# Attention and a two-layer network on one core: a new order of all engines, drawn with at most eight loads open, and one V load moved ahead of a K and a Q

## The chip, the cores and the metric

The kernel runs on one core of a Trainium2 chip. The metric is the device time of one execution in microseconds. Engines are called TensorE (PE, matmuls; PEld are its weight loads), VectorE (DVE), ScalarE (ACT), GpSimd (POOL) and SyncE (SP). All loads are issued by GpSimd, which converts float32 to float16 on the way; all stores are issued by SyncE, and some of the last by ScalarE too.

## The reference

Eight batches of attention with 12 heads, 448 tokens and 64 columns a head, then a network of two layers over the 3584 tokens:

```
scores = q @ k.T / sqrt(64);  attn = softmax(scores);  x = attn @ v     # 8 x 12 x (448, 64)
x = x laid out as (3584, 768)
h = x @ w_in            # w_in (768, 2048)
g = h * sigmoid(h)
out = g @ w_out         # w_out (2048, 768), out (3584, 768) float32
```

## The kernel before

**Work.** The 12 heads of a batch form three groups of four. A unit is a group of a batch; batch 0's groups are cut into two pieces of query tokens (7 times 32 each), so there are 6 + 21 = 27 units, numbered in that order (units 0 to 2 are the first pieces of batch 0, 3 to 5 the second ones, 6 to 8 the groups of batch 1). For each unit:

- K and Q are loaded (L322, L332) and transposed in 32 x 32 blocks on VectorE (L387, L398).
- Scores (L406): four heads side by side in four row tiles of 32 of the array, one chunk of keys at a time, into PSUM.
- Exponentials on ScalarE (L442), into tiles E.
- Sums over keys: VectorE adds tiles of E (L453), TensorE multiplies with ones (L483, or L497 in batch 0), VectorE transposes, inverts and spreads the sums (L542, L559, L570).
- E times V (L468) in column tiles of 32, and VectorE's scaling into xT (L607).

The first layer is computed block by block (L620), its gate by a tanh on ScalarE (L641) and a product on VectorE (L666). The last four batches are taken as two pairs with seven products instead of eight (L756), with additions on VectorE (L789) and ScalarE's copies and gates (L783, L802). The second layer is direct for the first four half tiles (L850, here called plain) and by seven products of sums for the rest (L837), with additions on VectorE (L829 for the operands, L890 for the results, L662 for sums of `w_out`).

On TensorE matmuls thus come in several tile shapes: full (128 x 128), column tiles of 32, row tiles of 32, and a few with 64. Until the first block of the first layer, matmuls with zeros (L1773) fill gaps that the plan foresees.

**What sets the order.** All instructions are written out by a planner. `Order` holds a clock, the time at which each engine is free, and lists of waiting operations for ScalarE and VectorE; each operation has a duration, dependencies and a bias. At each step ScalarE and VectorE take the ready operation with the lowest ready time plus bias; TensorE takes scores, attention or network blocks by rules of the main loop. When all is planned, the operations are emitted in order of planned start, and every engine runs its list in that order. The planned times thus decide the order, but the chip waits for semaphores, not for the plan.

**Loads.** `Order.load` estimates how long a load takes by its rows and bytes, with fixed extras for certain loads (`DMA_GAPS`, `more`). GpSimd's list is a queue in the order in which `plan_k`, `plan_q`, `plan_v`, `plan_w_in` and `plan_w_out` are called; its head waits in the plan for a free buffer only:

```
op.done = self.dma_free + DMA_TAIL          # planned landing
...
plan_k(1, 2)
plan_q(NB0 + 2)
for hg in range(NG):
    plan_v(1, hg, hg + 1)
plan_w_out(NFF // 2, 3 * NFF // 4)
```

In the built program of before, loads use eight semaphores in turn: every load from the ninth on waits until the load eight places before it has landed. This is so in both kernels. V of a unit is loaded in four pieces, by rows of 32 partitions (L352).

Of the kernel before, what the change touches and what calls it, by code (L numbers as in the profile page):

```python
# [18 lines left out]
HOP = 0.10  # L19
DMA_ROW = 0.004  # L20
DMA_RATE = 13400.0
DMA_GAPS = {1: 0.3, 3: 1.4}
FETCH = 5.6
DMA_START = 1.2
DMA_TAIL = 1.0


# [4 lines left out]
def act(n):  # L32
    return n * 0.000824 + 0.177


class Ring:


    def __init__(self, n, names=None):
        self.free = [(0.0, x) for x in (range(n) if names is None else names)]  # L40
# [54 lines left out]
class Order:  # L95


    def __init__(self, shy):
        self.now, self.shy = 0.0, shy
        self.free = {"PE": 1.0, "ACT": 2.1, "DVE": 1.2, "POOL": 1.2}  # L100
        self.wait = {"ACT": [], "DVE": []}
        self.pool = []
        self.dma_free, self.loads = 0.0, 0
        self.pe_n, self.fetched = 0, 0.0
        self.out = []
        self.mode, self.moe_mode = None, "full"
        self.steps = []
        self.busy = {e: 0.0 for e in self.free}
# [44 lines left out]
    def next_step(self):  # L153
        self.on_pe(self.steps.pop(0), self.moe_mode)

    def load(self, rows, row_bytes, emit, ring=None, gate=None, more=0.0):
        op = Op("POOL", 0.58, emit)
        self.loads += 1
        took = rows * (DMA_ROW + row_bytes / DMA_RATE) / 16 + DMA_GAPS.get(self.loads, more)
        self.pool.append((op, took, ring, gate))  # L160
        return op

    def step(self):

        soon = []
        for eng in ("ACT", "DVE"):
            if self.free[eng] > self.now:
                soon.append(self.free[eng])
                continue
            best, urgent = None, None  # L170
            for op in self.wait[eng]:
                at = op.ready()
                if at is None:
                    continue
                if at > self.now:
                    soon.append(at)
                    if op.bias <= -10 and (urgent is None or at < urgent):
                        urgent = at
                elif best is None or at + op.bias < best[0]:
                    best = (at + op.bias, op)  # L180
            if best and best[1].bias >= 0 and eng == "DVE" and urgent is not None:
                if urgent < self.now + self.shy * best[1].busy:
                    continue
            if best:
                self.wait[eng].remove(best[1])
                self.start(best[1])
                soon.append(self.free[eng])
        if self.free["POOL"] > self.now:
            soon.append(self.free["POOL"])
        elif self.pool:  # L190
            op, took, ring, gate = self.pool[0]
            at = 0.0
            if ring is not None:
                at = ring.when(1)
            if at is not None and gate is not None:
                g = gate()
                at = None if g is None else max(at, g)
            if at is not None and at <= self.now:
                self.pool.pop(0)
                if ring is not None:  # L200
                    ring.take()
                self.start(op)
                self.dma_free = max(self.dma_free, self.now + DMA_START) + took
                op.done = self.dma_free + DMA_TAIL
                soon.append(self.free["POOL"])
            elif at is not None:
                soon.append(at)
        return soon
# [3 lines left out]
def kernel(  # L212
# [13 lines left out]
    DFF = moe_w_in.shape[1]  # L226
    HG = 4
    NG = NH // HG
# [8 lines left out]
    NFF = DFF // 128  # L237
# [13 lines left out]
    COLD = 8.5  # L251
    FIRST = 47
    WHOLE = 7
    TANH_B = -2
    GATE_B = -6
    ADD_B = 1
    SUM_B = -3
    COPY_B = -2
    READ_B = -6
    PAIR_B = -6  # L260
    SILU_B = -1
    HOLD = 0.2
    TILED = 5
    QUART = 1
    JOIN = 0
    STRIPS = 80.0
    VFIRST = 3
    TURN = 4
    LOOK = 1
    SOON = -5  # L270
    KEEP = 0.3
    NBD = 3
    SHY = 0.5
    TWB = 8
    SXB = 8
    SURE = -1.3
    PIECES = ((0, 7), (7, TPP))
# [42 lines left out]
    def load_k(b, hg):  # L320
        t = sb.tile([128, TPP * D], FP16, name=f"rk_{b}_{hg}", tag="rk", bufs=NRK)
        nc.gpsimd.dma_start(out=t, in_=group_of(k, b, hg))  # L322
        rawk[(b, hg)] = t
# [36 lines left out]
    def load_w_in(c, f0, f1):  # L360
        nc.gpsimd.dma_start(
            out=w_in_t[:, 2 * c : 2 * c + 2, f0:f1],
            in_=moe_w_in[256 * c : 256 * (c + 1), f0:f1].rearrange(
                "(p j) f -> p j f", j=2
            ),
        )
# [552 lines left out]
    units = []  # L919
# [5 lines left out]
    od = Order(SHY)  # L925
# [7 lines left out]
    def plan_k(b, hg):  # L933
        ld_k[(b, hg)] = od.load(128, 2 * D * TPP, lambda: load_k(b, hg), rk_ring)

    def plan_q(n):
        g0, g1 = units[n][2:]
        ring = rq_ring if g0 == 0 else None
        ld_q[n] = od.load(128, 2 * D * (g1 - g0), lambda: load_q(n), ring)

    def plan_v(b, hg0, hg1):
        made = []
        for x in range(4):
            ring = v_ring if (x == 0 and b > 0) else None
            heads, toks = HG * (hg1 - hg0), X_TOK[form(b, hg0)][x][1]
            made.append(
                od.load(32 * heads, 2 * D * toks, lambda x=x: load_v(b, hg0, hg1, x), ring)
            )
        for hg in range(hg0, hg1):
            ld_v[(b, hg)] = made  # L950

    def plan_w_in(f0, f1):
        made = [
            od.load(256, 2 * (f1 - f0), lambda c=c: load_w_in(c, f0, f1), more=0.7 * (f0 + c == 0))
            for c in range(NG)
        ]
        for f in range(f0 // 128, f1 // 128):
            ld_win[f] = made

    def plan_w_out(f0, f1):  # L960
        wout_rows.append(f0)
        ld_wout.append(od.load(128 * (f1 - f0), 2 * DM, lambda: load_w_out(f0, f1)))

    NB0 = NG * len(PIECES)
    for hg in range(NG):
        if hg == VFIRST:
            plan_v(0, 0, 1)
        plan_k(0, hg)
        plan_q(hg)
    plan_v(0, int(VFIRST < NG), NG)  # L970
    plan_q(NG)
    if QUART:
        plan_w_in(0, DFF // 4)
        plan_q(NG + 1)
        plan_q(NG + 2)
        plan_w_in(DFF // 4, DFF // 2)
    else:
        plan_q(NG + 1)
        plan_q(NG + 2)
        plan_w_in(0, DFF // 2)  # L980
    plan_k(1, 0)
    plan_q(NB0)
    if QUART:
        plan_w_in(DFF // 2, 3 * DFF // 4)
        plan_w_in(3 * DFF // 4, DFF)
    else:
        plan_w_in(DFF // 2, DFF)
    plan_k(1, 1)
    plan_q(NB0 + 1)
    plan_w_out(0, NFF // 4)  # L990
    plan_w_out(NFF // 4, NFF // 2)
    plan_k(1, 2)
    plan_q(NB0 + 2)
    for hg in range(NG):
        plan_v(1, hg, hg + 1)
    plan_w_out(NFF // 2, 3 * NFF // 4)
    plan_w_out(3 * NFF // 4, NFF)
    for n in range(NB0 + NG, NU):
        b, hg = units[n][:2]
        plan_k(b, hg)  # L1000
        plan_q(n)
        plan_v(b, hg, hg + 1)

    turned = {"n": 0}

# [36 lines left out]
    def queue_ffn1(b, g0, g1):  # L1042
# [6 lines left out]
        for fs in turns:  # L1049

            def run(fs=fs):
# [4 lines left out]
                for i, f in enumerate(fs):  # L1056
# [15 lines left out]
                        [op],  # L1072
                        -3 if b == 0 else TANH_B,
                        tail=0.2,
# [42 lines left out]
    def plan_pair():  # L1117
        for todo in pair_todo[:8]:
# [9 lines left out]
            if qk_seq or od.pool or not e_ring.can(1, od.now):  # L1128
# [8 lines left out]
                    [pair_w[(k, f0)] for k in {2: (1,), 4: (2,)}.get(m, ())],  # L1137
                    TWB + f0,
                )
# [43 lines left out]
    def queue_pair_f(pb, f, xs):  # L1183
# [10 lines left out]

        def read(name, eng, fn, deps, then=None, bias=PAIR_B):
            busy = act(S) + 0.04 if eng == "ACT" else S / 960.0 + 0.155
# [5 lines left out]
        def gate_of(j, r, x, deps, then):  # L1202
            read((j, r), "ACT", lambda: silu(pb, f + HF * j, r, x), deps + silu_op, then, SILU_B)
            g_op.setdefault((pb + r, f + HF * j), []).append(done[(j, r)])
# [136 lines left out]
    def plan_sums():  # L1341
# [12 lines left out]
        for m in (5, 6, 7, 3):  # L1354
            sg_op[(qd, m)] = []
            n = HF if qd < WHOLE else HF // 2
            for f0 in range(0, HF, n):
                deps = [x for f in range(f0, f0 + n) for x in gates[f] + gates[f + HF]]
                if m != 5:
# [7 lines left out]
                            deps,  # L1367
                            SUM_B,
                        )
# [95 lines left out]
    def moe_ready():  # L1465

        soon, held = None, 0
        if av_data["at"] is not None and av_data["at"] <= od.now + HOLD:
            held = len(av_seq[0][0]) if av_seq[0][1] else 1
        if qk_data["at"] is not None and qk_data["at"] <= od.now + KEEP:  # L1470
            held += 1
# [315 lines left out]
    while True:  # L1787
# [9 lines left out]
        if od.free["PE"] <= od.now:  # L1797
# [8 lines left out]
            if qk is not None and qk <= od.now and (od.now >= pace["next"] or moe_i is None):  # L1806
                u0 = units[qk_seq[0][0][0]]
# [32 lines left out]
        if zb is not None and warm["on"] and od.free["PE"] <= od.now and wait > 0.06 and od.now > 0.9:  # L1840
            rate = 2350.0 if od.now > COLD else 1200.0
            n = int(wait * rate / 64) * 64 if od.now > COLD else int(wait * rate / 64 + 0.9) * 64
            if warm.pop("first", None):
                n = FIRST * 128
            n = max(n, 64)
            op = Op("PE", n / rate, lambda n=n, at=zb: run_zeros(n, at))
# [37 lines left out]
```

## Time and profile before

| what | value |
|---|---|
| median of 3 runs | 388.33 us (387.20 to 390.61) |
| the profiled execution | 386.79 us |
| its span in the trace | 385.0 us |
| TensorE busy | 377.3 us (98% of the span) |
| VectorE busy | 297.2 us (77%) |
| ScalarE busy | 244.1 us (63%) |
| GpSimd busy (issuing loads) | 88.0 us (23%) |
| granted TensorE clock | 0.994 on average |
| loads | 22.8 MB on GpSimd's queue |

The durations used below come from this one profiled execution, so sums are made against its own 386.79 us. Busy shares are averages over stages: start-up (to about 22 us), batch 0 and the loading of both weight matrices (to about 75 us), attention of the other batches between network blocks (to about 245 us), and the paired batches with the last products (to the end). Starts of matmuls are recorded, their ends are modelled. In brackets at the end of a timeline line stand the idle time of the engine ahead of that instruction and what ended it. A line such as L352 is a line of the kernel before; where the change shifts lines, the same operation stands 7 lines further down ahead of the planning part and 12 lines further up behind it.

### The profile page before, as it was taken

The page shows a single profiled execution, that of the slowest core. Times are in us where ns is not written, and L with a number is a line of the kernel's source. Part 1 is how long each engine was busy: PE and PEld are TensorE (multiplying, and loading weights), DVE is VectorE, ACT ScalarE, POOL GpSimd, SP SyncE. Part 2 cuts the span into 40 slices and gives each one's busy share as a digit, 9 for nine tenths or more (in the row PEclk, how much of TensorE's full clock was granted, in tenths as well). Part 3 has the DMA queues.
Part 4 walks back from the last instruction along what each step waited for, and adds up shares of the span by engine and source line. Part 5 has one row for each costly group of instructions (what it writes and reads, how often), then busy time and mean ns, then how long its engine had stood idle before and what let it go on. Part 6 is the DMA issues. An engine that isn't in the chain of part 4 may idle for free.

```text
span 385.0 us, 12240 instructions
## 1 busy us (share of the span) xinstructions
PE 377.3 (98%) x5184; PEld 197.6 (51%) x5184; DVE 297.2 (77%) x549; ACT 244.1 (63%) x381; POOL 88.0 (23%) x159
## 2 busy tenths in 40 slices
PE   7999998999999999999999999999999999999996
PEld 3567763444444444445444445555556655555663
DVE  2558677898889898898978788989788647777662
ACT  3888895798868588886667978136871037872000
POOL 7564364602324426050335000000000000000000
PEclk9899999999999999999999999999999999999999
DMA  7999999951919596447594301120002330001343
GB/s 116 200 206 208 171 157 211 145 100 21 127 33 168 90 173 83 65 62 113 104 179 59 48 3 44 44 66 16 2 0 68 94 84 5 0 2 43 94 105 90
DMA packets 37222, 34.61 MB, mean 90 GB/s; under 512 B 11696, under 2 KB 37168, under 8 KB 37168
## 3 DMA queue, kind: packets, MB, share of 16 engines
q0 software_dynamic: 26416, 22.82, 40.1%
q1 hardware_dynamic: 9984, 10.24, 9.8%
q10 hardware_dynamic: 768, 0.79, 0.8%
q8 instruction: 40, 0.66, 0.7%
q14 instruction: 14, 0.11, 0.1%
HBM read 45.61 MB, written 11.01 MB: 147 GB/s over the span
## 4 chain that ended last, share of the span: by engine, by line
PE 86%; DMA 8%; DVE 2%; POOL 1%; issue 1%; ACT 0%; ACTq 0%; POOLq 0%
PE P L837 31%; PE P L756 16%; PE P L620 15%; PE P L406 10%; PE P L468 9%; DMA rq<-in_q_dram 8%; PE P L850 2%; PE P L1773 2%; PE P L483 1%; POOL V L352 1%; PE P L497 0%; DMA out_dram<-ost 0%; POOL rk L322 0%; DVE G L666 0%; DVE rq L398 0%
## 5 line engine op out<-in xcount | busy, mean ns | idle before, releaser
L442 ACT ACTIVATE E<-P 128x448 f16<-128x448 f32 (+4 forms) x172 | 153.1, 918 | 49.1 <-PE P L406 47.5
L620 PE MATMUL P<-xT,w_in_t 128*32 128x448 f16 (+2 forms) x1236 | 82.1, 339 | 0.0
L352 POOL DMA_DIRECT2D V<-in_v_dram x84 | 46.1, 562 | 90.0 <-PE P L468 65.9
L620 PEld LDWEIGHTS <-w_in_t 128*32 128x32 f16 (+1 forms) x1236 | 45.2, 97 | 34.2 <-issue 14.7
L837 PEld LDWEIGHTS <-G 128*32 128x32 f16 (+1 forms) x928 | 39.7, 97 | 27.9 <-issue 4.8
L406 PE MATMUL P<-rq,KT 32*128 32x448 f16 (+4 forms) x864 | 51.0, 342 | 2.3 <-DVE rq L398 2.0
L666 DVE SCALAR_TENSOR_TENSOR G<-G,P 128x448 f16<-128x448 f16 x64 | 38.4, 607 | 12.0 <-ACT G L641 11.2
L837 PEld LDWEIGHTS <-S 128*32 128x32 f16 (+1 forms) x648 | 30.9, 97 | 21.7 <-issue 2.7
L837 PE MATMUL P<-D,G 128*32 128x384 f16 (+1 forms) x448 | 38.9, 326 | 0.0
L837 PE MATMUL P<-w_out_t,S 128*32 128x384 f16 (+1 forms) x424 | 38.9, 326 | 0.0
L641 ACT ACTIVATE G<-P 128x448 f16<-128x448 f32 x64 | 34.6, 544 | 2.6 <-PE P L620 1.9
L890 DVE TENSOR_TENSOR ost<-P,u 128x384 f32<-128x384 f32 x39 | 21.5, 551 | 18.8 <-PE P L837 15.7
L837 PE MATMUL P<-w_out_t,G 128*32 128x384 f16 (+1 forms) x480 | 35.0, 327 | 0.0
L468 PE MATMUL P<-E,V 128*32 128x448 f16 (+2 forms) x672 | 34.9, 355 | 0.0
L756 PE MATMUL P<-sx,tw 128*128 128x448 f16 x144 | 30.8, 352 | 0.0
L406 PEld LDWEIGHTS <-KT 32*128 32x128 f16 (+2 forms) x864 | 14.6, 99 | 29.1 <-issue 25.8
L756 PEld LDWEIGHTS <-tw 128*128 128x128 f16 x192 | 18.8, 98 | 17.5
L607 DVE SCALAR_TENSOR_TENSOR xT<-P,R 128x448 f16<-128x448 f32 x42 | 24.2, 614 | 4.2 <-PE P L468 4.0
L387 DVE STREAM_TRANSPOSE KT<-rk 128x256 f32<-128x256 f32 (+3 forms) x48 | 16.6, 383 | 10.6 <-DMA rk<-in_k_dram 8.8
L468 PEld LDWEIGHTS <-V 128*32 128x32 f16 (+2 forms) x672 | 14.7, 95 | 18.9 <-issue 10.4
L894 ACT COPY u<-P 128x384 f32<-128x384 f32 x13 | 6.2, 479 | 26.1 <-PE P L837 21.1
L453 DVE TENSOR_TENSOR T<-T,E 128x1792 f16<-128x1792 f16 x20 | 21.7, 1083 | 0.4
(80 smaller groups left out, 450.6 us busy)
## 6 DMA issues: line engine op xcount, KB each, us to landing
out_dram<-ost SPq DMA_DIRECT2D x208, 48.0 KB, 1.7
rk<-in_k_dram POOLq DMA_DIRECT2D x24, 224.0 KB, 5.4
rq<-in_q_dram POOLq DMA_DIRECT2D x21, 224.0 KB, 5.5
w_in_t<-in_moe_w_in_dram POOLq DMA_DIRECT2D x12, 256.0 KB, 8.7
w_out_t<-in_moe_w_out_dram POOLq DMA_DIRECT2D x4, 768.0 KB, 11.4
V<-in_v_dram POOLq DMA_DIRECT2D x43, 64.0 KB, 3.9
V<-in_v_dram POOLq DMA_DIRECT2D x40, 48.0 KB, 4.2
out_dram<-ost ACTq DMA_DIRECT2D x16, 48.0 KB, 1.8
```

Source lines behind the costliest of these rows:

```text
L352: nc.gpsimd.dma_start(out=VT[(b, hg0)][32 * x : 32 * (x + 1), :, 0:count, :], in_=v[b, hs].rearrange("h (i g) d -> i h g d", g=TPP)[:, :, ...
L406: nc.tensor.matmul(out=P[p0 : p0 + 32 * (x1 - x0), pS[h], at : at + nq], lhsT=KT[(b, hg)][32 * h : 32 * (h + 1), c, x0:x1, :, e], rhs=QT[n ...
L442: nc.scalar.activation(out=E[(n, w)][0:kr, h0:h1, 0:nk], in_=P[0:kr, bank : bank + h1 - h0, 0:nk], func=AF.Exp, scale=attn_scale,)
L453: nc.vector.tensor_tensor(out=T[n], in0=T[n] if step else E[(n, 0)], in1=E[(n, step + 1)], op=ALU.add,)
L468: nc.tensor.matmul(out=a[32 * h : 32 * (h + 1), 0:nq], lhsT=w, rhs=e[k0:k1, h, at : at + nq], start=start, stop=stop, skip_group_check=True,)
L607: nc.vector.scalar_tensor_tensor(out=xc(b, cc)[:, 32 * g0 : 32 * g1], in0=acc[(n, part)][:, 0:nq], scalar=0.5, in1=rdn_t[n].rearrange("p g ...
L620: nc.tensor.matmul(out=h_t[(b, f, t0)][m0:m1, 0 : t1 - t0], lhsT=w_in_t[:, cc, 128 * f + m0 : 128 * f + m1], rhs=xc(b, cc)[:, t0:t1], star ...
L641: nc.scalar.activation(out=g, in_=h, func=AF.Tanh)
L666: nc.vector.scalar_tensor_tensor(out=g, in0=g, scalar=1.0, in1=h, op0=ALU.add, op1=ALU.mult)
L756: nc.tensor.matmul(out=pp_t[(*key, PBANK[m])], lhsT=w[:, c, :], rhs=xc(pb + x[0], 3 * x[1] + c) if isinstance(x, tuple) else sx_t[(pb, x)] ...
L837: nc.tensor.matmul(out=pr_t[(qd, BANK[m])][m0:m1, 0:OH], lhsT=w[:, f, m0:m1], rhs=W_[m][:, f, :], start=(f == 0 and BANK[m] == m), stop=(f ...
L890: nc.vector.tensor_tensor(out=out, in0=a, in1=b, op=op)
```

## The change

The planner's picture of the loads is replaced. `Order.load` keeps every load in a list; a load may be issued in the plan only 0.28 us after the load eight places before it has landed (`LANES`, `LANE`). The fixed extras of single loads give way to pauses at six planned times (`DMA_PAUSES`), and a load of more than 128 rows begins later by 0.0044 us for each further row. The order of the loads is written as a list, in which `u` stands for K and Q of a unit (Q alone for units 3 to 5), `v` for V, `i` for a quarter of `w_in` and `o` for a quarter of `w_out`. Read against the order before, one item has moved: `v3`, V of batch 1's first group, stands ahead of `u8`, that batch's last K and Q, not behind it. Some biases change: tanh -2 to -1, sums of the second layer's operands -3 to 1, additions of the pairs -6 to -2, gates of the pairs -1 to -0.3, sums of `w_in` for the pairs 8 to 4, and two margins for holding PSUM banks (`HOLD`, `KEEP`) become 0. Since all of this feeds the planner, the order on every engine is another one from about 47 us on; what is computed is the same.

```diff
-DMA_GAPS = {1: 0.3, 3: 1.4}
+DMA_PAUSES = ((0.0, 0.3), (4.0, 1.35), (15.5, 0.9), (21.0, 0.7), (48.5, 0.8), (65.0, 0.8))
+LANES = 8
+LANE = 0.28
+DMA_START_ROW = 0.0044
...
-    def load(self, rows, row_bytes, emit, ring=None, gate=None, more=0.0):
+    def load(self, rows, row_bytes, emit, ring=None):
         op = Op("POOL", 0.58, emit)
-        self.loads += 1
-        took = rows * (DMA_ROW + row_bytes / DMA_RATE) / 16 + DMA_GAPS.get(self.loads, more)
-        self.pool.append((op, took, ring, gate))
+        n = len(self.loads)
+        self.loads.append(op)
+        took = rows * (DMA_ROW + row_bytes / DMA_RATE) / 16
+        lane = self.loads[n - LANES] if n >= LANES else None
+        begin = DMA_START + DMA_START_ROW * max(0, rows - 128)
+        self.pool.append((op, took, ring, lane, begin))
         return op
...
-            if at is not None and gate is not None:
-                g = gate()
-                at = None if g is None else max(at, g)
+            if at is not None and lane is not None:
+                at = None if lane.done is None else max(at, lane.done + LANE)
             if at is not None and at <= self.now:
...
-                self.dma_free = max(self.dma_free, self.now + DMA_START) + took
+                self.dma_free = max(self.dma_free, self.now + begin)
+                while self.pauses and self.pauses[0][0] <= self.dma_free:
+                    self.dma_free += self.pauses.pop(0)[1]
+                self.dma_free += took
                 op.done = self.dma_free + DMA_TAIL
...
-    TANH_B = -2
+    TANH_B = -1
...
-    SUM_B = -3
+    SUM_B = 1
...
-    PAIR_B = -6
-    SILU_B = -1
-    HOLD = 0.2
+    PAIR_B = -2
+    SILU_B = -0.3
+    HOLD = 0
...
+    LOADS = "u0 u1 u2 v0 u3 i0 u4 u5 i1 u6 i2 i3 u7 o0 o1 v3 u8 v4 v5 o2 o3"
...
-    KEEP = 0.3
+    KEEP = 0
...
-    TWB = 8
+    TWB = 4
...
+    rest = LOADS.split()
     for n in range(NB0 + NG, NU):
-        b, hg = units[n][:2]
-        plan_k(b, hg)
-        plan_q(n)
-        plan_v(b, hg, hg + 1)
+        rest += [f"u{n}", f"v{n - NG}"]
+    for what in rest:
+        plan(what)
```

The calls in the plan of before that this list takes the place of are left out here, as is `plan`, which calls `plan_k`, `plan_q`, `plan_v`, `plan_w_in` or `plan_w_out` by an item's letter.

More of the change, by code (lines that the diff above doesn't have):

```diff
@@ L102, in __init__ @@
         self.pool = []
-        self.dma_free, self.loads = 0.0, 0
+        self.dma_free, self.loads, self.pauses = 0.0, [], list(DMA_PAUSES)
         self.pe_n, self.fetched = 0, 0.0
@@ L190, in step @@
         elif self.pool:
-            op, took, ring, gate = self.pool[0]
+            op, took, ring, lane, begin = self.pool[0]
             at = 0.0
@@ L253 @@
     WHOLE = 7
-    TANH_B = -2
+    TANH_B = -1
     GATE_B = -6
     ADD_B = 1
-    SUM_B = -3
+    SUM_B = 1
     COPY_B = -2
     READ_B = -6
-    PAIR_B = -6
-    SILU_B = -1
-    HOLD = 0.2
+    PAIR_B = -2
+    SILU_B = -0.3
+    HOLD = 0
     TILED = 5
-    QUART = 1
     JOIN = 0
     STRIPS = 80.0
-    VFIRST = 3
+    LOADS = "u0 u1 u2 v0 u3 i0 u4 u5 i1 u6 i2 i3 u7 o0 o1 v3 u8 v4 v5 o2 o3"
     TURN = 4
@@ L953, in plan_w_in @@
         made = [
-            od.load(256, 2 * (f1 - f0), lambda c=c: load_w_in(c, f0, f1), more=0.7 * (f0 + c == 0))
+            od.load(256, 2 * (f1 - f0), lambda c=c: load_w_in(c, f0, f1))
             for c in range(NG)
@@ L964, with plan @@
     NB0 = NG * len(PIECES)
[L965 to L997, printed above, removed]
+    def plan(what):
+        kind, at = what[0], int(what[1:])
+        if kind == "u":
+            b, hg = units[at][:2]
+            if at < NG or b:
+                plan_k(b, hg)
+            plan_q(at)
+        elif kind == "v":
+            plan_v(at // NG, at % NG, NG if at == 0 else at % NG + 1)
+        elif kind == "i":
+            plan_w_in(DFF // 4 * at, DFF // 4 * (at + 1))
+        else:
+            plan_w_out(NFF // 4 * at, NFF // 4 * (at + 1))
+    rest = LOADS.split()
     for n in range(NB0 + NG, NU):
-        b, hg = units[n][:2]
-        plan_k(b, hg)
-        plan_q(n)
-        plan_v(b, hg, hg + 1)
+        rest += [f"u{n}", f"v{n - NG}"]
+    for what in rest:
+        plan(what)
     turned = {"n": 0}
```

## The prediction

> **What bounds the kernel now.** I read the page's busy times first, then the slices, then the waits of TensorE (PE), then the order of instructions around each wait.
>
> ```profile
> span 385.0 us, 12240 instructions
> ...
> PE 377.3 (98%) x5184; PEld 197.6 (51%) x5184; DVE 297.2 (77%) x549; ACT 244.1 (63%) x381; POOL 88.0 (23%) x159
> ...
> PEclk9899999999999999999999999999999999999999
> DMA  7999999951919596447594301120002330001343
> ```
>
> TensorE is the bound from end to end, at full granted clock from the third slice on, while the transfers are full only in the first eight slices (9.6 us each). "98%" does not say that TensorE streams all the time, because ends of matmuls are modelled. So I took the starts. Inside a run of one tile shape they lie 189, 163 or 96 ns apart for 448, 384 or 224 columns (tiles of 32 rows or columns run four or eight side by side and share one such slot). All matmuls but the zero fillers make 339.2 us by these spacings. The other 46 us of the 385 are, in time: 14 to 15 us until about 22 us, when loads come in and fillers run; then 0.11 to 0.15 us (I take 0.12) at each change of tile shape, of which the whole trace has 212; 3.8 us from the last matmul's end to the end of the span; and real waits. After the start-up I find only these waits, by spacing beyond a slot and a shape change: 0.41 us at 60.8, 0.92 at 63.8, 0.28 at 92.1, about 0.6 in pieces from 201.6 to 205.4, and 0.25 at 284.4. **Together 2.5 us.** From 250 us on there is nothing else to take. The two waits at 60 and 64 us are on loads, as the timeline says:
>
> ```profile
> 60.81 1.46 PE L850 MATMUL P<-w_out_t,G 128*128 128x384 f16 x8 [0.25 <-DMA w_out_t<-in_moe_w_out_dram]
> ...
> 63.12 0.65 DVE L398 STREAM_TRANSPOSE rq<-rq 128x448 f32<-128x448 f32 x1 [0.53 <-DMA rq<-in_q_dram]
> ...
> 63.81 0.58 PE L406 MATMUL P<-rq,KT 32*128 32x448 f16 x8 [0.86 <-DVE rq L398]
> ```
>
> The first waits for the last quarter of `w_out` (landed 60.77), the second for batch 2's first Q (landed 63.09) and its transpose, 0.65 us. GpSimd's timeline shows why these loads come late:
>
> ```profile
> 33.34 0.56 POOL L352 DMA_DIRECT2D V<-in_v_dram  x1 [0.45 <-DMA w_in_t<-in_moe_w_in_dram]
> ...
> 40.58 0.55 POOL L352 DMA_DIRECT2D V<-in_v_dram  x1 [3.20 <-DMA w_out_t<-in_moe_w_out_dram]
> 44.38 0.54 POOL L352 DMA_DIRECT2D V<-in_v_dram  x1 [3.26 <-DMA w_out_t<-in_moe_w_out_dram]
> 45.46 0.54 POOL L352 DMA_DIRECT2D V<-in_v_dram  x1 [0.54 <-DMA rk<-in_k_dram]
> ...
> 49.33 1.51 POOL L369 DMA_DIRECT2D w_out_t<-in_moe_w_out_dram  x2
> ```
>
> Each load from the ninth on already waits for the load eight places before it. The planner of before does not know that, and so planned these products and scores for a time at which their data was not there.
>
> **The change, part by part.** *Matmuls.* Counted in the two programs, the work is the same: no matmul but fillers differs in columns. 16 product matmuls become four tiles of 32 columns and 6 first-layer ones become one of 128; both forms take the same slot. Shape changes are 213 instead of 212: +0.12. Fillers have 16,128 columns instead of 16,000: 128 more at 96 ns per 224 columns, +0.05. Real matmuls stand in the same order until about 47 us, so the start-up stays as it is; ScalarE's exponentials run back to back from 12.4 to 21.3 us there, in the same order. Sum: **+0.17**.
>
> *Loads.* The four loads of V (batch 1, group 0) go ahead of K and Q (batch 1, group 2) on POOL's queue; the other loads keep their order. In before the second `w_out` load landed at 44.10, that K at 45.18, that Q at 46.37, and V's pieces at 46.61, 47.00, 47.33 and 47.51: 1.14 us for the four. Moved, V is there at 45.2, K at 46.3, Q at 47.5. V's first matmul stands in the new order 1.4 us earlier (its place by spacings and shape changes is 47.5 instead of 49.0; the trace ran 0.3 later than that reckoning here), so about 2.6 us of cover. The scores of that K and Q stand at 51.5; after Q's landing and its transpose on DVE (0.63) 3.7 us are left for whatever DVE does first. The moved loads take the lanes of the two K and Q loads, so the V loads behind them wait for landings of V, not K and Q: the third `w_out` load can issue from about 48.2 instead of 49.33, an estimate from these landings. I take nothing for it; it could bring 1.1 us of earlier landing.
>
> *Orders.* With loads modelled later, the plan puts the third `w_out` quarter's first use at 59.9 instead of 57.5, the fourth's at 63.3 instead of 60.05, and batch 2's first scores at 65.4 instead of 62.1. Even with landings unchanged (57.01, 60.77, 63.09 and 0.65 of transpose), these leave 2 us or more. So the waits at 60.8 and 63.8 go: **-1.33**. What is late next? Later K loads have more: batch 2's second K is landed by 65.3 and used at 73.7. In exchange attention runs 3 to 6 us later through batches 2 to 7, with first-layer blocks and products earlier. DVE's list moves with it: the time of its operations ahead of each sum-transpose (L542) grows by 1.0 to 4.3 us in batches 2 to 7, that of TensorE's list ahead of the sums by 3.3 to 6.8, and at each of them by at least 1.5 more than DVE's. Less the 1.3 us that TensorE no longer waits, DVE meets them no later than now, if barely in the tightest. The remaining 1.1 us of waits (92, 202 and 284 us) come from DVE or ScalarE; a new order may lose them or find others. They bound this from below at -1.1; from above I have no row but the whole seam below, +3.2. I take 0.
>
> **Sum:** -1.33 + 0.17 = -1.16 on the profiled execution's own 386.79 us: 385.6. The median of the three runs shown, 388.33, lies 1.54 above that execution, and even their lowest (387.20) lies above it; the same step from the median is 387.2. I take **386.5**, between the two, 0.5% under the median. Something like 1% is what a measurement of this kernel can tell from no change.
>
> **Rivals.** *A, a new wait at the seam, slower.* This is the end of attention and the start of the paired batches, where DVE is nearly full:
>
> ```profile
> 232.00:245.00 13.00, 13.00 (x312) 7.28 (x308) 11.65 (x19) 6.91 (x11) 0.00 (x0) 1.00 0.18 48
> 245.00:258.00 13.00, 13.00 (x88) 7.26 (x81) 11.71 (x19) 3.77 (x7) 0.00 (x0) 1.00 0.20 51
> ```
>
> (The third number after TensorE's and the weight loads' busy time is DVE: 11.65 and 11.71 of 13.) In the new order the last sums come 3.8 us later and the first pair product 3.0 us earlier, 241.6. From the last sums to the first pair addition TensorE now has 14.8 us of matmuls, where it had 17.9. Before, DVE's way from that L542 (240.21) to that addition (258.27) took 18.06 us: 27 operations, 18.81 us of durations, which overlap a little. If it took as long again, TensorE would wait 18.06 - 14.8 = 3.2 us: 388.8. Against it: the new list has 27 operations with 15.22 us of durations there, 13.2 us with the same overlap of 0.08 each. It decides when DVE needs over 14.8. Chance 0.14; in about half of that, waits come in more than one place and it passes 1%.
>
> *B, the plan holds but nothing is gained.* The two load waits are replaced by equal ones (banks, or ScalarE, which now takes first-layer functions in twos between exponentials: 1.29 + 0.54 + 2 x 0.54 = 2.9 us a step). Time: 386.8 + 0.2 = 387.0. Chance 0.16.
>
> *C, each V load pays a start of its own.* A V load issued to an idle queue (93.50) landed 2.61 us later (96.11). Four of these in a row after 44.10 give 54.5; its matmuls would wait some 6.7 us: 392.3. Against it: behind other loads the same four landed 0.18 to 0.39 us apart. Chance 0.02. In the Trainium skill, "DMA: Bandwidth & Descriptors", section "Anatomy of one DMA", a load is fitted as 2.0 us plus its bytes at 436 GB/s; by that, in series, four pieces would take 8.6 us, and the wait would be about 5 us. The spacing of 0.18 to 0.39 us in this trace does not bear that out for loads that are queued; the section itself puts most of the fixed part into the receipt, not the moving.
>
> *D, more gain.* All waits after start-up go and the loads' pauses shorten too: 386.8 - 2.5 + 0.2 = 384.5. To pass 1% (3.9 us), start-up would have to shrink as well, and its order is unchanged. Chance 0.08, over 1% in 0.04.
>
> **Numbers.** Forecast (0.5 to 2 us gained) 0.60; B 0.16; A 0.14; D 0.08; C 0.02. The range goes from D's 384.5 to A's 388.8 plus 0.9, a quarter of the 3.4 us over which the three runs spread: **384.5 to 389.7**. Faster by over 1%: 0.04; slower by over 1%: C and half of A, 0.09; within 1%: 0.87.
>
> **What would show it.** Right: no load wait before L850's counterpart near 60 and 63 us, batch 2's first scores without a wait on a transpose, V of batch 1's first group landed by 45.5, 213 shape changes, the last matmul about 1.2 us earlier. A: TensorE idle or with wide spacings between 240 and 260 us, ended by a DVE addition. C: V's pieces 2 us apart. Wrong altogether would be a wait in the middle batches (100 to 220 us), where my reckoning compares sums of durations and not each single wait.

## The result, and the profile after

| | before | after |
|---|---|---|
| median of 11 runs each, on one chip | 387.99 us (386.17 to 390.61) | 384.17 us (383.60 to 386.09) |
| ratio, 95% interval | | 0.9924 (0.9895 to 0.9952) |
| the profiled execution | 386.79 us | 383.95 us |
| its span | 385.0 us | 382.2 us |
| last matmul ends | 381.16 us | 378.34 us |

The changed kernel is faster by 0.8% (0.5 to 1.1%). The middle of this lies within the 1% that the prediction called "no change", and it is on the side that it named. The ratio is an estimate with an interval, not the quotient of the two medians, which would be 0.990. The 386.5 was 2.3 us too high, and 384.17 lies 0.3 us below the lower end of the range; taken as a share, 0.9924 of the 388.33 that the prediction started from is 385.4 us, inside it.

First the busy times and slices, from the page of the changed kernel:

```profile
span 382.2 us, 12302 instructions
...
PE 376.3 (98%) x5213; PEld 196.9 (52%) x5213; DVE 297.7 (78%) x549; ACT 243.6 (64%) x381; POOL 88.1 (23%) x159
...
PEclk9999999999999999999999999999999999999999
DMA  7999999920939283919394401310002330001443
```

TensorE is the bound as before. The second slice's clock of 8 is gone; the second profile of the kernel before doesn't have it either, so it is no property of the change (below). The stretch that the prediction was about, on TensorE's timeline of the changed kernel (start, duration, engine, line, operation; an idle time would stand in brackets):

```profile
55.80 2.12 PE L857 MATMUL P<-w_out_t,G 128*128 128x384 f16 x12
...
58.39 2.12 PE L857 MATMUL P<-w_out_t,G 128*128 128x384 f16 x12
...
61.12 2.77 PE L857 MATMUL P<-w_out_t,G 128*128 128x384 f16 x16
63.83 0.57 PE L413 MATMUL P<-rq,KT 32*128 32x448 f16 x8
```

L857 is L850's counterpart and L413 is L406's. The products with the third quarter of `w_out` start at 58.39. Those with the fourth start within the last run of L857, at 61.79: by the semaphores in the trace, its fifth matmul is the first one that waits for that load. Batch 2's first scores start at 63.83. No line has a bracket: nothing is waited for. The quarters landed at 55.20 and 59.01, Q at 61.28. The time from a landing to the first use of what landed is called cover here; it is 3.2 us for the third quarter, 2.8 for the fourth and (less Q's transpose of 0.63 to 0.65) 1.9 for Q.

GpSimd's timeline of the changed kernel shows the moved V:

```profile
30.61 0.55 POOL L359 DMA_DIRECT2D V<-in_v_dram  x1
...
35.84 0.55 POOL L329 DMA_DIRECT2D rk<-in_k_dram  x1 [0.81 <-DMA rk<-in_k_dram]
...
44.37 3.80 POOL L359 DMA_DIRECT2D V<-in_v_dram  x7 [3.42 <-DMA w_out_t<-in_moe_w_out_dram]
48.13 1.53 POOL L376 DMA_DIRECT2D w_out_t<-in_moe_w_out_dram  x2
```

V's four pieces are issued from 30.61 on, ahead of K at 35.84. They landed at 44.26, 44.56, 44.93 and 45.11, K at 46.23 and Q at 47.31. The third quarter of `w_out` could be issued at 48.13, where it had been 49.33.

A wait that is left looks like this (TensorE's timeline and its list of waits, of the changed kernel; in the list stand total, times and longest in us):

```profile
93.09 1.63 PE L475 MATMUL P<-E,V 64*32 64x448 f16 x32 [0.23 <-DVE xT L614]
```

```profile
PE P L475 <- DVE xT L614: 0.5, 2, 0.2
```

By the starts of matmuls (spacing beyond a slot and a shape change, as in the prediction) these waits of attention on VectorE are 0.29 at 93.1, 0.29 at 149.2, 0.28 at 205.2 and 0.28 at 224.7; with 0.27 at 281.6 they make 1.4 us, 0.3 more than the 1.1 of the kernel before.

**Where the 2.8 us came from, in these two profiles.** The first block of the first layer starts at 21.56 us, where it started at 23.44 (-1.88); the two load waits are gone (-1.33); shape changes and fillers (+0.17); other waits (+0.3). This makes -2.7 of the -2.8 that the last matmul's end moved; 0.1 is left without a place. So two thirds of the gain seen in these two profiles lie in the start-up, whose order the change does not touch, and yet the medians differ by more than 2.8 us. This is what the experiments had to clear up.

### The profile page after: what moved, and what is told of

Its sections match the earlier page's. It is cut to its first block, busy times and chain, and to the rows that moved or that the text cites. A ratio compares the mean times of both kernels' runs of the same rounds, so it can differ in the third digit from the quotient of the medians.

```text
span 382.2 us, 12302 instructions
## 1 busy us (share of the span) xinstructions
PE 376.3 (98%) x5213; PEld 196.9 (52%) x5213; DVE 297.7 (78%) x549; ACT 243.6 (64%) x381; POOL 88.1 (23%) x159
## 4 chain that ended last, share of the span: by engine, by line
PE 97%; DVE 1%; DMA 0%; ACT 0%; issue 0%; SPq 0%; ACTq 0%
PE P L844 31%; PE P L627 20%; PE P L763 17%; PE P L413 11%; PE P L475 10%; PE P L857 3%; PE P L1761 3%; PE P L490 2%; PE P L504 1%; DMA out_dram<-ost 0%; DVE xT L614 0%; DVE ost L897 0%; ACT E L449 0%; ACT R L790 0%; SPq L892 0%
## 5 line engine op out<-in xcount | busy, mean ns | idle before, releaser
L627 PE MATMUL P<-xT,w_in_t 128*32 128x448 f16 (+2 forms) x1218 | 82.0, 339 | 0.0
L627 PEld LDWEIGHTS <-w_in_t 128*32 128x32 f16 (+1 forms) x1218 | 45.1, 97 | 34.1 <-issue 15.1
L413 PE MATMUL P<-rq,KT 32*128 32x448 f16 (+4 forms) x864 | 50.6, 342 | 0.3 <-ACT E L449 0.3
L673 DVE SCALAR_TENSOR_TENSOR G<-G,P 128x448 f16<-128x448 f16 x64 | 38.4, 609 | 9.9 <-ACT G L648 9.2
L413 PEld LDWEIGHTS <-KT 32*128 32x128 f16 (+2 forms) x864 | 14.3, 99 | 27.0 <-issue 24.4
L460 DVE TENSOR_TENSOR T<-E,E 128x1792 f16<-128x1792 f16 x20 | 21.6, 1078 | 0.6 <-ACT E L449 0.4
```

The source lines that it names most:

```text
L413: nc.tensor.matmul(out=P[p0 : p0 + 32 * (x1 - x0), pS[h], at : at + nq], lhsT=KT[(b, hg)][32 * h : 32 * (h + 1), c, x0:x1, :, e], rhs=QT[n ...
L460: nc.vector.tensor_tensor(out=T[n], in0=T[n] if step else E[(n, 0)], in1=E[(n, step + 1)], op=ALU.add,)
L627: nc.tensor.matmul(out=h_t[(b, f, t0)][m0:m1, 0 : t1 - t0], lhsT=w_in_t[:, cc, 128 * f + m0 : 128 * f + m1], rhs=xc(b, cc)[:, t0:t1], star ...
L673: nc.vector.scalar_tensor_tensor(out=g, in0=g, scalar=1.0, in1=h, op0=ALU.add, op1=ALU.mult)
```

## The experiments

Two theories stood at first. **The loads:** the load waits set the time of the kernel before, whatever the start-up does; the start-up difference of the two profiles is chance. **The start-up:** the new kernel starts earlier as a rule, and the load waits are the small term of 1.3 us that the prediction took. For the parts of the change there were three more: the planner's new picture of the loads (**the model**), the place of V, and the seven biases and margins (that these, and the other order which they draw, bring the gain is the rival O). Ratios below are to the kernel before, run beside each kernel on the same chip, with 95% intervals.

### Both kernels once more

No edit. Run e1 is the kernel before:

> The kernel of before, unchanged, profiled once more. Theory L (the gain is the two load waits at 60 and 64 us, 1.3 us, and the 1.9 us by which the first block of the first layer starts earlier in the profile after, 21.56 against 23.44, is chance of that one execution): the start-up of this execution may differ from the first by a microsecond or two, with the first Q landing anywhere from 5.5 to 6.5 us, and the load waits near 60 to 64 us are there again. Rival S (the change shortens the start-up): the first block starts at 23.4 again, within 0.3 us. Time: 1.00 of before.

Measured: 386.67 us, ratio 0.9986 (0.9959 to 1.0013). Run e2 is the changed kernel:

> The changed kernel, unchanged, profiled once more. Theory L: the first block of the first layer may start anywhere between 21.5 and 23.5 us, no wait on loads at 59 to 66 us. Rival S: it starts at 21.6 again, within 0.3 us. Time: 0.992 of before.

Measured: 384.41 us, 0.9925 (0.9899 to 0.9952). The gain repeats. The second profile of the kernel before, span 387.1 us, is the more telling one. TensorE's timeline:

```profile
58.41 1.46 PE L850 MATMUL P<-w_out_t,G 128*128 128x384 f16 x8 [2.63 <-DMA w_out_t<-in_moe_w_out_dram]
...
62.21 1.46 PE L850 MATMUL P<-w_out_t,G 128*128 128x384 f16 x8 [1.04 <-DMA w_out_t<-in_moe_w_out_dram]
...
65.04 0.58 PE L406 MATMUL P<-rq,KT 32*128 32x448 f16 x8 [0.69 <-DVE rq L398]
...
75.03 0.55 PE L406 MATMUL P<-rq,KT 32*128 32x448 f16 x5 [0.74 <-DVE xT L607]
```

This execution's first block started at 21.25 us, 2.2 us earlier than in the first profile of the same kernel, and even 0.3 earlier than in the changed kernel. So the early start-up isn't a property of the change: the second theory falls. And it brought nothing: TensorE came to the third quarter of `w_out` early and waited for it. By the starts the four waits are 2.79, 1.21, 0.74 and 0.98, **5.72 us instead of 1.33**. Two things changed at once between the two profiles: TensorE came 2.2 us earlier, and the two quarters landed 1.4 us later (58.37 and 62.17 instead of 57.01 and 60.77). In the first profile the late start-up had covered the third quarter entirely, and most of the wait for the fourth.

Against this profile the sum closes: start-up +0.31, the four waits -5.72, shape changes and fillers +0.17, other waits +0.4 (1.0 to 1.4) make -4.84; the last matmul ends 4.90 earlier in the changed kernel (383.24 to 378.34).

### The biases alone

Run e3 is the kernel before, with `TANH_B`, `SUM_B`, `PAIR_B`, `SILU_B`, `HOLD`, `KEEP` and `TWB` as in the change:

```diff
-    TANH_B = -2
+    TANH_B = -1
...
-    SUM_B = -3
+    SUM_B = 1
...
-    TWB = 8
+    TWB = 4
```

> The kernel of before with the seven new biases and margins alone (tanh, sums, pairs, gates, two margins, sums of w_in); loads and their model as before. By its order the load waits stay (third and fourth w_out quarter first used at 57.5 and 60.05, batch 2's first scores at 62.1, as before), 213 shape changes. Theory L: 1.000 of before, within 0.003. Rival O (the gain is the order of ScalarE and VectorE): 0.993.

Measured: 1.0022 (0.9998 to 1.0046). TensorE's list of waits:

```profile
PE P L850 <- DMA w_out_t<-in_moe_w_out_dram: 1.2, 2, 1.0
...
PE P L406 <- DVE rq L398: 0.7, 1, 0.7
```

The load waits are all there: 0.34, 1.21 and 0.75 by the starts, 2.3 us in all. The biases alone bring nothing.

### V alone

Run e4 is the kernel before, with only the load moved:

```diff
+plan_v(1, 0, 1)
 plan_k(1, 2)
 plan_q(NB0 + 2)
-for hg in range(NG):
+for hg in range(1, NG):
     plan_v(1, hg, hg + 1)
```

> The kernel of before with V of batch 1's first group loaded ahead of that batch's last K and Q, and nothing else changed (old model of loads, old biases). By its order the fourth w_out quarter is used at 59.9 and batch 2's first scores stand at 62.65, 0.5 us later than before; the landings come about 1.1 to 1.8 us earlier as they do in the profile after. Theory L: the load waits shrink from 1.3 to under 0.3 us, 214 shape changes: 0.997 of before. Rival M (the plan's better model of loads is what counts): 1.000.

Measured: 386.93 us, 1.0000 (0.9976 to 1.0025), a miss: I had expected a gain. TensorE's list of waits:

```profile
PE P L468 <- DVE xT L607: 0.9, 1, 0.9
PE P L406 <- DVE rq L398: 0.6, 1, 0.6
PE P L850 <- DMA w_out_t<-in_moe_w_out_dram: 0.5, 1, 0.5
```

The loads do land earlier, the fourth quarter at 58.87. But the planner, which doesn't know that a load waits for the one eight places before it, puts the products at about the old times. Waits of 0.56 and 0.64 (by the starts) stay, and in this trace a new one on VectorE, 1.25 at 69.5, takes back what that gained against e3. Ahead of it VectorE had itself waited 1.48 us for a load of K.

### The model and V, without the biases

Run e5 is the changed kernel, with the seven numbers set back:

> The changed kernel with the old biases and margins: the new model of loads and the moved V, nothing else. By its order the loads' first uses are those of the changed kernel (fourth w_out quarter 63.3, batch 2's first scores 65.4 by spacings), 211 shape changes instead of 213. Theory L (load waits are the whole gain): 0.992 of before, as the changed kernel, 0.2 us less. Rival O (the biases carry part of it): 0.995 or more.

Measured: 384.03 us (383.08 to 385.49), 0.9912 (0.9885 to 0.9939): the whole gain. Behind the start-up there is no wait on a load in its trace, although this profile happens to have the late start-up (first block at 23.43) and still a span of 383.7 us. The kernel before had 385.0 with the same start-up: the difference of 1.3 us is the size that the prediction gave.

### V set back

Run e6 is the changed kernel with its own model and biases, and `u8 v3` in the old order:

```diff
-LOADS = "... o0 o1 v3 u8 v4 v5 o2 o3"
+LOADS = "... o0 o1 u8 v3 v4 v5 o2 o3"
```

> The changed kernel with V of batch 1's first group back behind K and Q, all else as changed. Its order has 221 shape changes instead of 213 (8 x 0.12 = 1.0 us more), puts the fourth w_out quarter at 65.0 and batch 2's first scores at 68.6. Theory L: no load waits near 60 us, so 0.9925 of before plus 1.0 us of shape changes: 0.995. Rival V (the moved V is what frees the loads): load waits near 60 us come back, 0.998 or more.

Measured: 384.75 us (383.80 to 386.49), 0.9950 (0.9922 to 0.9977), as expected. No wait on a load near 60 us either: the plan uses the loads later by itself. It has 221 shape changes instead of 213, which at 0.12 is 1 us. The full change measured 0.9924, 0.9925 and 0.9938, so by the middle values V's place is worth 0.5 to 1 us; the intervals overlap, and it may be worth nothing. What runs e3 to e6 don't take apart is the model itself: the rule of eight open loads, the pauses and the later begin of large loads came together in each run that has it.

In the executions profiled without an added load, the third quarter landed at 57.01, 58.37, 56.07 and 55.72 with V behind K and Q, and at 54.91 to 55.89 in eight with V ahead: earlier by 1.4 us in the mean. The prediction took nothing for it, and named 1.1. Whether V's place is the cause is open. The 55.72 is that of e6, the only one of the four with the new model; it lies among the eight, and e6 issued this load at 48.33, the seven with V ahead and the new model at 48.0 to 48.5.

### A load more

To see what cover is worth, runs e7 and e8 have one load more (384 KB into a tile that is written over before it is read) ahead of the third quarter:

```diff
     def load_w_out(f0, f1):
+        if f0 == NFF // 2:
+            nc.gpsimd.dma_start(
+                out=W_[4][:, 0:4],
+                in_=moe_w_out[0:512, 0:OH].rearrange("(f p) m -> p f m", p=128),
+            )
```

In the kernel before (e7):

> The kernel of before with one more load of 384 KB (part of w_out, into a buffer that is written over later), issued ahead of the third w_out quarter and not known to the planner: the order of all other work is the same. It takes about 1.9 us of the transfers' time by the 3.8 us of 768 KB. Theory L (before, loads set the time at 58 to 64 us): the load waits grow by the 1.9 us whole, 1.005 of before. Rival N (loads have cover): 1.000.

Measured: 388.49 us against 386.64 beside it, 1.0035 (1.0003 to 1.0067). In the changed kernel (e8):

> The changed kernel with the same load more. Theory L: by the landings of its second profile the fourth w_out quarter has 2.2 us of cover and batch 2's first Q 1.3 us, so only 0.6 us of the 1.9 are paid: 0.994 of before, against 0.9925 without it. Rival N: 0.9925. If the whole 1.9 us shows (0.997), cover is not what the change brought.

Measured: 384.58 us, 0.9944 (0.9918 to 0.9971), against 0.9925 for the changed kernel itself on another chip. TensorE's lists of waits, first of the kernel before with the load, then of the changed one with it (the added lines shift the numbers by 5: L855 is L850, L411 and L418 are the scores, L480 is attention, L632 the first layer):

```profile
PE P L855 <- DMA w_out_t<-in_moe_w_out_dram: 2.7, 2, 1.7
PE P L411 <- DVE rq L403: 2.0, 3, 1.0
...
PE P L411 <- DVE R L547: 0.9, 1, 0.9
```

```profile
PE P L418 <- DVE rq L410: 1.0, 2, 0.6
PE P L632 <- DVE G L678: 0.5, 1, 0.5
PE P L480 <- DVE xT L619: 0.5, 2, 0.2
```

In the changed kernel the fourth quarter now lands at 61.17, 1.5 to 2.5 us later than in the seven traces of this order of loads without the added one (58.68 to 59.70). Its products start at 62.43 without a wait; cover of 1.6, 1.3 and 0.4 us is left at the third quarter, the fourth and Q. A start-up 0.6 us later than in the first profile of the changed kernel gives a part of that. Of the 1.0 us on transposed Q, all lies in the start-up. The 0.5 at L632 is a wait at 146 us, to which the last experiment comes back. So the trace supports the theory of the loads: a lateness of this size is taken up by the cover. The times can't tell it as clearly: 0.9944 against 0.9925 is a step of 0.2%, the kernel before took one of 0.35%, and each interval is 0.3% wide to either side. Nor does the one trace of e7 show what the kernel before pays: its third quarter landed at 57.81, inside the span of landings without the load, and its waits on the loads are no longer than in e1.

### The start-up

One course of the start-up costs time. In two of fourteen traces (the first of the kernel before, and e5) the first block starts at 23.4 us, in the others at 21.2 to 22.4. Two things come together in those two: batch 0's first Q lands at 6.5 us and not, as in all others but e6, at 5.4 to 5.7, so that TensorE idles 1.1 and 0.8 us ahead of the first scores, and 1.7 and 2.3 us after these begin the granted clock is halved for 3.4 us. Windows over that time (stretch, its length, then busy time of TensorE, weight loads, VectorE, ScalarE and GpSimd, granted clock, share of the transfer engines, GB/s), the kernel before and the changed one:

```profile
8.60:12.10 3.50, 3.50 (x27) 1.67 (x30) 1.41 (x4) 2.33 (x3) 2.66 (x5) 0.51 1.40 190
```

```profile
8.60:12.10 3.50, 3.50 (x56) 1.63 (x51) 2.22 (x8) 3.50 (x5) 2.85 (x5) 1.00 1.36 186
```

27 matmuls instead of 56 in the same 3.5 us, at 0.51. The late Q alone isn't enough: in e6 it landed at 6.56 too, TensorE idled 0.7 us, the clock stayed full, and the first block started at 22.24. In the Trainium skill, "TensorE: Matmul & The Clock Gate", section "What's actually happening", the clock is said to be decided anew in windows of 4096 cycles at 1.2 GHz, 3.41 us, which run freely; the length agrees with each of the halved stretches here (3.4 us each).

What tells these executions apart is seen in the 3.4 us behind the first rise of the clock, which comes at 3.8 to 7.0 us. The same windows for e5 and e6, from the rise on:

```profile
5.89:9.30 3.41, 2.33 (x38) 1.59 (x37) 1.41 (x4) 1.68 (x3) 2.20 (x4) 1.00 1.13 160
9.30:12.72 3.42, 3.42 (x32) 1.17 (x30) 1.12 (x3) 2.29 (x4) 2.36 (x5) 0.50 1.43 184
```

```profile
6.16:9.58 3.42, 2.43 (x39) 1.72 (x39) 1.41 (x4) 1.92 (x3) 2.18 (x4) 1.00 1.16 169
9.58:12.99 3.41, 3.41 (x52) 1.56 (x51) 2.39 (x7) 3.35 (x5) 2.17 (x4) 1.00 1.47 189
```

TensorE is busy there for 1.78 us in e10 (below), 1.99 in the first profile of the kernel before and 2.33 in e5, and the clock is halved next; in the other eleven traces it is busy for 2.43 us (e6) or more, and the clock stays full. How much idle time falls into this stretch depends on its length and on when the clock rose. The ends of matmuls are modelled, and the fourteen traces were sorted afterwards, so a border between 2.33 and 2.43 is a reading of them and not a tested rule.

Two runs changed the zero fillers ahead of the first scores in the changed kernel, e9 by 1024 columns more:

```diff
     def run_zeros(n, bank):
+        n += 1024 if n == FIRST * 128 else 0
```

> The changed kernel with the first run of zero fillers 1024 columns longer (7040 instead of 6016, at half clock up to about 7.0 us), the order of everything else the same. Theory G (start-up takes one of two courses: where the first Q lands at 6.5 us, as in the first profile of before, TensorE idles 1.1 us, the granted clock falls back to half for 3.4 us, and the first block of the first layer starts at 23.4 instead of 21.3): the fillers bridge the gap, the clock stays full after it has risen, first block at about 22.2 us in every execution, 0.993 to 0.994 of before. Rival Q (the late Q itself costs the time, the clock nothing): as the changed kernel, 0.9925, plus 0.7 us where Q is early.

and e10 by 2048 fewer:

> The changed kernel with the first run of zero fillers 2048 columns shorter (3968, done at about 4.5 us), the order of everything else the same. Theory G: TensorE idles from 4.5 us to the first scores in every execution; the clock rises later or falls back for 3.4 us, and the first block starts at 23 us or later: 1 to 2 us more than the changed kernel, 0.996 of before. Rival Q: no difference, 0.9925.

Measured: with more, 384.36 us (383.59 to 384.81), 0.9928 (0.9899 to 0.9957), the same as the changed kernel. The Q of its trace landed early, at 5.50, so it doesn't show a gap being bridged. With fewer, 386.09 us (384.86 to 386.90), 0.9973 (0.9950 to 0.9996): 1.7 us slower than with more, on the same chip. The profile of that execution has the halved stretch, though its Q landed early, at 5.42 (windows ahead of it and over it):

```profile
4.40:7.80 3.40, 1.77 (x33) 1.31 (x34) 1.00 (x3) 1.23 (x2) 2.66 (x5) 1.00 1.07 160
7.80:11.20 3.40, 3.40 (x30) 1.31 (x26) 2.03 (x6) 2.10 (x3) 1.93 (x3) 0.50 1.30 181
```

So idle time of TensorE ahead of the first scores, here 1.35 us that the missing fillers leave, can bring the halved clock without a late Q. That section of the Trainium skill has the clock fall after a window that is idle; in this trace TensorE was busy for 1.77 of the 3.40 us ahead, so one that is half idle was enough. But it doesn't explain the whole loss. The first block started at 22.41, not at 23 or later as expected. And of the twelve executions timed, the six whose mean clock was below 0.997 had a median of 385.50, the six at full clock 386.40. What slows those six isn't shown. The granted clock is recorded from its first rise on (4.42 us in this trace; ahead of it fillers of 512 columns start 0.43 us apart, where 448 columns take 0.19 at full clock), so a rise that came late would not lower the mean; no trace has one. In the kernel before, 9 of the 101 executions timed beside e1 to e12 had a mean clock below 0.997, with a median of 389.41 against 386.61 for the rest; in the changed kernel none of 31 had. Since the start-up's order is the same in both, I count that as no proof of a difference.

### The best version

Run e11 has the model and V's place, the old biases, and 1024 columns more of fillers:

> The new model of loads and the moved V with the old biases, and the first run of fillers 1024 columns longer. 211 shape changes (0.2 us less than the changed kernel), no fall of the clock in start-up. Theory L with G: 0.9915 to 0.993 of before, a narrow spread as with the longer fillers in the changed kernel; not to be told from the changed kernel. If the two gains added up (no fall of the clock, fewer changes), 0.990 or less.

Measured: 383.65 us (383.14 to 384.41), 0.9908 (0.9875 to 0.9942). Beside it the changed kernel once more (e12):

> The changed kernel once more, beside the run above on the same chip: 0.9925 of before. Its start-up should be one of the two courses: first block of the first layer at 21.2 to 22.2 us with the clock full throughout, or near 23.4 us with the clock at half for 3.4 us; from about 30 us on, waits as in its first two profiles (at 93, 149, 205, 224 and 281 us) and none on loads.

Measured: 384.74 us (383.74 to 386.52), 0.9938 (0.9908 to 0.9967). The version beats both kernels in the median, the changed one by 1.1 us; the two intervals overlap.

The trace of e12 has a wait that was not expected. VectorE's timeline, then TensorE's (L405 is the transpose of Q, L673 the gate's product, L627 the first layer):

```profile
144.70 0.65 DVE L405 STREAM_TRANSPOSE rq<-rq 128x448 f32<-128x448 f32 x1 [2.04 <-DMA rq<-in_q_dram]
145.27 0.58 DVE L673 SCALAR_TENSOR_TENSOR G<-G,P 128x448 f16<-128x448 f16 x1
```

```profile
145.91 0.94 PE L627 MATMUL P<-xT,w_in_t 128*32 128x448 f16 x16 [0.99 <-DVE G L673]
```

VectorE waits 2.04 us for a Q that landed at 144.68. The gate's product stands behind that Q in VectorE's list, and TensorE waits for the product: 1.15 us by the starts. In e8 it is the same place, 0.65 us. In all six traces of the new order with the new biases (both profiles of the changed kernel, e8, e9, e10 and e12) VectorE waits for this Q, for 0.84 to 2.04 us, and TensorE is reached in two of them. In the five traces of the old model and in e5, e6 and e11 VectorE doesn't wait for a Q there. So the changed kernel still has a wait on a load of varying length, in another place, and it may be part of why the old biases do no worse than the new ones; no run tests that.

## Why the prediction was right, and what it mis-sized

- **The load waits go: right, and the mis-sized term.** The step "-1.33" priced the waits as one profile shows them. The runs show 1.33 and 5.72 us (0.98 of it a wait on VectorE that comes with them) for the same kernel, since a late start-up hides them and late landings add to them, and 2.3 us in e3. The gain between the medians was 3.8 us in the first comparison and 2.1 to 2.8 in two later ones (387.24 or, in e1, 386.67 to 384.41; 386.82 to 384.74); the prediction's 1.16 fits only the execution that it was read from, whose start-up was the late one. With that same late start-up the change without its biases was 1.3 us shorter in span.
- **"Even with landings unchanged these leave 2 us or more": right in what it led to**, and it is the step that carries the result. Covers of 3.2, 2.8 and 1.9 us were there, and in e8 1.6, 1.3 and 0.4 were left. But in the changed kernel's first profile both sides had moved: the first uses came 1.5 us ahead of the places named, as the start-up was early, and the landings came 1.8 us earlier. Against the landings of the kernel before, these first uses would have had 1.4, 1.0 and 0.1 us.
- **The earlier issue of the third quarter, taken at nothing: too low.** It issued at 48.13 (48.2 was named), and landed 1.4 us earlier in the mean. But in e4 an earlier landing alone gained nothing, and e6 issued it at 48.33 without the moved V, so the reason given, the lanes that V takes, is not shown.
- **Start-up stays as it is: right.** The 1.88 us between the two profiles are no property of the change, as e1 and e5 show.
- **Shape changes +0.12, fillers +0.05, V at 45.2, K at 46.3, Q at 47.5: right** (213 changes; 45.11, 46.23, 47.31).
- **Other waits, taken as unchanged: 0.3 us too good in the first profile, more in others.** 1.4 us of them stand in the new order, all but one on VectorE's last step of attention. The sign that the prediction gave for "wrong altogether", a wait in the middle batches, is there: 0.29 at 149.2, 0.28 at 205.2, and 1.15 at 145.9 in e12. Comparing sums of VectorE's durations could not show it, for in e12 VectorE itself waits for a load.
- **Rival A, the seam: did not come.** From the last sums, transposed at 241.18, to the first pair addition, at 256.02, 14.84 us went by, just the matmuls that TensorE has there, and TensorE doesn't idle. VectorE's list there has 21 operations, not the 27 of the prediction; their durations, 15.19 us, are as it said, and with their overlap they take 13.88. The windows that the prediction showed, in the changed kernel:

```profile
232.00:245.00 13.00, 13.00 (x299) 6.83 (x295) 10.81 (x18) 6.27 (x9) 0.00 (x0) 1.00 0.25 64
245.00:258.00 13.00, 13.00 (x92) 7.05 (x85) 12.42 (x20) 4.31 (x8) 0.00 (x0) 1.00 0.20 53
```

  VectorE is busy for 12.42 of 13 us in the second, where it was 11.71: the reserve is thin, as the prediction said, and it held.
- **Rival B** (nothing gained) is excluded by the interval. **Rival C** too: V's pieces landed 0.18 to 0.37 us apart. **Rival D** named 384.5, nearest to the time measured, but for another reason: it had all waits go and the transfers' pauses shorten. By e1 there was more load wait to be lost, and 1.4 us of other waits stayed.
- **The median:** between the steps from 386.79 and from 388.33 I took the middle for the result. The runs of the kernel before spread over 4.4 us in the first comparison, those of the changed one over 2.5. That spread could have been read as a sign of a wait of varying length on the path; that the lost waits are what narrowed it is argued from e1 and e8, not shown by a run of its own.

**What stays open:** why the first transposed Q lands at 5.4 or at 6.5 us; why the third quarter of `w_out` lands anywhere from 55.7 to 58.4 us with V behind K and Q; which part of the model moves the first uses; what slows the full-clock executions of e10; and whether the new biases cost anything beside the model (0.9912 without, 0.9924 with).

## What to carry to other kernels

A wait on a load has no fixed price. In one profile it is the landing less the engine's arrival, and any chance delay ahead of it hides it; so compare landings and arrivals over two profiles, and price the wait by the earliest arrival and the latest landing that they show. Where an order is planned and then run in lists, the planner must expect the loads when they come: moving a load without a better picture of them gained nothing (1.0000), and the picture with the load in its old place gained 0.5%. That the limit of eight open loads is the part that counts is likely, but not tested alone. Some 2 to 3 us of cover at the first uses near 60 us went with a faster kernel, and a further load of 384 KB could be added at no price that the runs can tell. A new order moves every first use, though: look for the loads that lost their cover, here a Q at 144 us, also where the engine that waits for them is not the one that sets the time.

## What the runs showed of the hardware that was not expected

- The halved clock for one stretch of 3.4 us after TensorE had idled only 0.8 to 1.35 us ahead of the first scores. In the 3.4 us behind the clock's rise TensorE was busy for 1.78 to 2.33 us in the three traces that have it, and for 2.43 or more in the eleven that don't.
- The same load of the same kernel, 768 KB at the same place in the queue, landed 1.4 us apart in two executions (57.01 and 58.37), though it was issued 0.6 us earlier in the one in which it landed later.
